# Choosing the best 80 tokens per expert of the first 16 tiles before attention has ended

## The chip, the cores and the metric

The kernel runs on one core of a Trainium2 chip. The metric is the time of one execution on the device in microseconds (us); smaller is better. The engines are TensorE (PE; its weight loads are PEld), VectorE (DVE), ScalarE (ACT), GpSimd (POOL) and SyncE (SP, which only issues transfers). Each works through its own queue in order.

## The reference

Sliding-window attention with sinks feeds a mixture of experts with a capacity.

```
q, k, v: [4, 8, 768, 64]        # 3072 tokens of 512 values come out of it
keep   = (key < 4) | (0 <= query - key < 128)
x      = softmax(where(keep, q @ k.T / 8, -1e9)) @ v     -> x[3072, 512]
logits = x @ w_gate                                      # [3072, 8]
expert = argmax(logits); gate_w = softmax(logits)[expert]
for e in 8 experts:
    tok = tokens of e; if more than 80: the 80 with the largest gate_w
    out[tok] = gate_w[tok] * (relu(x[tok] @ w1[e]) @ w2[e])   # w1 512x1024, w2 1024x512
out of every other token = 0
```

## The kernel before, in words

The 3072 tokens are 24 tiles of 128 rows. Attention runs in 48 ticks: a tick is two units of two heads, and four ticks make the rows of two tiles (at the end, two ticks make one tile). The kernel writes the order of the engines' instructions itself (`manual_schedule`): in tick n stand `scores(n)` on PE, `softmax(n)` on DVE and `exps(n)` on ACT, then `transposes(n-1)`, and `weighted(n-2)`, the product with v. A calendar (`at`, `run`) hangs the work of the finished tiles on later ticks: turning x back into rows (`rows_turn`, `rows_keep`, `rows_scale`) and writing them to DRAM (`rows_write`), the gate (`gate_products`, `gate_logits`, `gate_exp`, `gate_hit`, `gate_keys`), and the table from which tokens are later picked (`gate_picks`).

A token's key is its gate weight times a power of two of its expert, so that one comparison of keys ranks within an expert and between experts. For a tile i, `keys_turn` and `keys_keep` put its keys as a row into `krow`. `rank_compare` (DVE) compares the keys of tile i with `krow` in pieces of up to 768 columns, from column 0 to the tile's own end: each piece gives, per token, how many come before it (`parts`). The piece that holds the tile itself is a scalar_tensor_tensor with `ties` (L737), the others are tensor_scalars (L740). The same 0/1 matrix, summed over rows by a PE matmul (`rank_count`), gives the other direction, for the tokens of the columns. `rank_count_last` does that for the last tile with one-column matmuls.

After the last tick two drain ticks and a tail follow: the last tiles' gates, the remaining comparisons, the offsets of the experts (`owed`, `off`, `ot`, `os`), the rank of every token (L969), one-hot rows of the slots (`hot`, L974), 24 matmuls that pick token number and gate for 8 experts x 80 slots (`pi`, L977), the index (L985, L986) and eight indirect DMAs that gather the rows (L998). 14 matmuls (L996) run on PE while it waits. Then per expert: 64 + 64 matmuls of the first product (`ph`, L1042), 64 + 64 of the second (`py`, L1057), and an indirect DMA that scatters the result (L1085).

The weights are 32 tiles of 1 MB, each four transfers of 256 KB on SP's queue (`load_weight`, L296), in the order in which the experts need them. 6 tiles are loaded during attention. 7 get their memory from the q, k and v tiles when attention ends, 4 from its work tiles, and the last 15 wait for a tile that has been used up. SP issues a transfer only when the one eight places before it in its queue has landed.

## Time and profile before

| | |
|---|---|
| median of 3 runs | 322.52 us (322.12 to 324.51) |
| the profiled execution | 325.12 us, its span 323.4 us |
| first softmax of tick 34 and of tick 47 on DVE | 133.82 and 187.96 us |
| first gather starts | 219.73 us |
| first and last expert matmul | 227.72 and 316.7 us |
| busy: PE, DVE, ACT, POOL | 286.3, 180.4, 158.0, 165.7 us |

Times in rows are counted from the start of the span. A row of a timeline gives start, duration, engine, line, operation, output and inputs, and in brackets how long the engine was idle before it and what ended that.

### The profile page before, as it was taken

Reading aid. Unit: us, or ns where it says so; the run is one execution under the profiler, and the core shown is the slowest. Engines: PE = TensorE matmul, PEld = TensorE weight load, DVE = VectorE, ACT = ScalarE, POOL = GpSimd, SP = SyncE. Lnnn points to the kernel's source line nnn. Section 1 sums busy time; section 2 is a strip of 40 time slices with the busy share of each in tenths; the row PEclk is TensorE's granted clock in tenths of the full one; section 3 lists DMA queues with packets and bytes.
Section 4 is the critical chain, followed back from the end, with each engine's and each line's share of the span. In section 5 each row is a group of like instructions: output and inputs, shape, how many; then the busy total and the mean of one; then the engine's idle time right before and its main releaser. Section 6 shows DMA issues by size and latency. Waiting matters only on the chain.

```text
span 323.4 us, 10862 instructions
## 1 busy us (share of the span) xinstructions
PE 286.3 (89%) x4232; PEld 229.2 (71%) x4232; DVE 180.4 (56%) x576; ACT 158.0 (49%) x631; POOL 165.7 (51%) x365
## 2 busy tenths in 40 slices
PE   7498999999989999999999997556898999989992
PEld 2365787877767777877776675242887998978981
DVE  6355877696887888889989989970010000000000
ACT  0655797777877687867777562100011112111210
POOL 4396687758997587967676756616400110011002
PEclk9589999999999999999999999756799999999997
DMA  6999133599462799753450001999999697766801
GB/s 189 324 325 413 38 131 130 198 284 312 184 241 73 218 301 412 277 162 131 133 199 32 2 35 39 320 358 347 298 367 373 195 357 206 239 205 184 311 26 49
DMA packets 32745, 69.68 MB, mean 215 GB/s; under 512 B 4272, under 2 KB 5296, under 8 KB 32304
## 3 DMA queue, kind: packets, MB, share of 16 engines
q1 hardware_dynamic: 31376, 65.78, 61.0%
q0 software_dynamic: 1024, 2.62, 2.6%
q8 instruction: 35, 0.57, 0.7%
q10 hardware_dynamic: 288, 0.52, 0.4%
q14 instruction: 22, 0.18, 0.2%
HBM read 55.02 MB, written 13.89 MB: 213 GB/s over the span
## 4 chain that ended last, share of the span: by engine, by line
PE 59%; DVE 12%; ACT 9%; DMA 7%; issue 5%; POOL 5%; SPq 1%; POOLq 0%; DVEq 0%; ACTq 0%
PE ph L1042 12%; PE py L1057 12%; PE sc L499 11%; DMA w<-in_moe_w_dram 7%; PE xp L593 7%; PE pp L552 6%; ACT prob L536 5%; DVE gt L740 3%; PE pl L648 3%; ACT pt L564 2%; DVE sc L519 2%; DVE nm L526 2%; PE warm L412 1%; PE bank_t L754 1%; PE pr L622 1%
## 5 line engine op out<-in xcount | busy, mean ns | idle before, releaser
L536 ACT ACTIVATE prob<-sc,nm 128x132 f32<-128x132 f32 (+1 forms) x192 | 69.0, 377 | 4.6 <-DVE nm L526 4.3
L499 PE MATMUL sc<-k,q 64*128 64x260 f32 (+1 forms) x384 | 59.1, 411 | 8.7 <-ACT prob L536 8.2
L1085 POOL DMA_INDIRECT out_dram<-y,idx x8 | 7.4, 921 | 82.3 <-ACT y L1074 71.9
L564 ACT COPY pt<-pp 128x512 f32<-128x512 f32 x48 | 28.1, 586 | 41.3 <-PE pp L552 34.8
L499 PEld LDWEIGHTS sc<-k,q 64*128 64x128 f32 x384 | 30.5, 190 | 25.0 <-ACT prob L536 16.8
L1042 PE MATMUL ph<-xs,w 128*64 128x80 f32 x1024 | 40.0, 238 | 5.6 <-issue 4.4
L1030 DVE COPY xs<-px 128x320 f32<-128x320 f32 x8 | 3.9, 492 | 73.4 <-PE px L1028 65.2
L519 DVE COPY_PREDICATED sc<-upper,sc 128x256 f32<-128x256 int8 x80 | 33.7, 422 | 18.1 <-PE sc L499 9.5
L526 DVE TENSOR_REDUCE nm<-sc 128x2 f32<-128x264 f32 (+1 forms) x96 | 41.4, 431 | 3.3
L1042 PEld LDWEIGHTS ph<-xs,w 128*64 128x64 f32 x1024 | 38.3, 141 | 6.8 <-issue 6.0
L536 ACT ACTIVATION_READ_ACCUMULATOR prob<-sc,nm 128x1 f32 x192 | 40.6, 211 | 0.0
L1057 PE MATMUL py<-h,w 128*64 128x80 f32 x1024 | 38.3, 234 | 1.0 <-ACT yt L1065 0.6
L572 POOL TENSOR_SCALAR_AFFINE_SELECT own<-pt 128x512 f32<-128x512 f32 (+1 forms) x48 | 28.1, 585 | 21.2 <-ACT pt L564 20.4
L1057 PEld LDWEIGHTS py<-h,w 128*64 128x64 f32 x1024 | 36.5, 137 | 2.9 <-issue 2.1
L593 PE MATMUL xp<-pt,v 128*64 128x128 f32 x384 | 37.1, 286 | 0.0
L740 DVE TENSOR_SCALAR_CACHE_REDUCE gt<-krow,keys 128x768 bf16<-128x768 f32 x36 | 35.5, 1005 | 0.0
L552 PEld LDWEIGHTS pp<-ident,prob 128*128 128x128 f32 x192 | 20.8, 144 | 16.5 <-issue 11.8
L552 PE MATMUL pp<-ident,prob 128*128 128x128 f32 x192 | 32.3, 292 | 0.0
L593 PE MATMUL xp<-own,v 128*64 128x128 f32 x320 | 31.1, 273 | 0.0
L1044 ACT ACTIVATE h<-ph 128x320 f32<-128x320 f32 x16 | 7.0, 437 | 46.3 <-PE ph L1042 46.3
L579 POOL TENSOR_SCALAR_AFFINE_SELECT pt<-pt 128x512 f32<-128x512 f32 (+1 forms) x48 | 27.8, 579 | 3.3
L632 POOL TENSOR_TENSOR xr<-xr,rs 128x512 f32<-128x512 f32 x24 | 25.6, 1067 | 5.2 <-ACT xr L627 5.0
(136 smaller groups left out, 461.8 us busy)
## 6 DMA issues: line engine op xcount, KB each, us to landing
w<-in_moe_w_dram SPq DMA_DIRECT2D x128, 256.0 KB
v<-in_v_t_dram SPq DMA_DIRECT2D x12, 512.0 KB
out_dram<-zeros SPq DMA_DIRECT2D x24, 256.0 KB
q<-in_q_t_dram SPq DMA_DIRECT2D x11, 512.0 KB
x_rows<-xr SPq DMA_DIRECT2D x22, 256.0 KB
k<-in_k_t_dram SPq DMA_DIRECT2D x3, 1584.0 KB
k<-in_k_t_dram SPq DMA_DIRECT2D x1, 1056.0 KB
vst_raw<-in_vs_t_dram SPq DMA_DIRECT2D x4, 256.0 KB
```

The lines of the kernel that those rows point to most:

```text
L499: pe.matmul(sc[:, h, c0:c0 + w], qs[g][r, hp, j % 2 * P:(j % 2 + 1) * P], ks[b][r, hp, k0:k0 + w], start=True, stop=True)
L519: ve.copy_predicated(own, upper, sc[:, :, 0:P])
L526: ve.tensor_reduce(out=nm, in_=sc[:, :, lo_c:hi_c], axis=AX.X, op=ALU.max, negate=True)
L536: ac.activation(prob[:, a, h, p0:], sc[:, h, lo_c:hi_c], AF.Exp, bias=nm[:, h:h + 1], scale=1.0, accum_out=ssum[:, n, 2 * hp + h:2 * hp + ...
L552: pe.transpose(pp[:, a, h], prob[:, a, h, SINK:], ident)
L564: ac.copy(pt, st.pop((t, "pp")))
L572: po.affine_select(out=own[:, a0:], in_=pt[:, a0:], pattern=[[0, 2 - a0], [0, 2], [1, P]], compare_op=ALU.is_ge, fill=0.0, base=0, channel ...
L579: po.affine_select(out=pt[:, a0:], in_=pt[:, a0:], pattern=[[0, 2 - a0], [0, 2], [-1, P]], compare_op=ALU.is_gt, fill=0.0, base=0, channel ...
L593: pe.matmul(xp[h * D:(h + 1) * D, a * P:(a + 1) * P], val[:, (2 * hp + h) * D:(2 * hp + h + 1) * D], pr[:, a, h], start=False, stop=(a == ...
L740: ve.tensor_scalar(gt[:, 0:w], krow[:, c0:c0 + w], keys[:, i:i + 1], None, ALU.is_ge, ALU.add, accum_out=ra)
L1042: pe.matmul(ph[m * D:(m + 1) * D, f], columns(0, e, c, fc * P + m * D), x[:, c], start=(c == 0), stop=(c == DC - 1), skip_group_check=True)
L1057: pe.matmul(to[m * D:(m + 1) * D, dc], columns(1, e, k, dc * P + m * D), h[:, k], start=(k == 0), stop=(k == HC - 1), skip_group_check=True)
```

## The change

Tiles 0 to 15 (`CUT`) are ranked among themselves during ticks 34 to 42, and the best 80 per expert are chosen there: `kept_hot` (one-hot slots), `kept_pick` (16 matmuls), `kept_keys` (their keys from the picked gates) and `kept_row_turn` put the 640 chosen keys into `kept_row`. A later tile is compared with the columns from 2048 on and with the 640 columns of `kept_row`, and no longer with columns 0 to 2047. In ticks 34 to 38 up to three comparisons are made per tick (`quick`). The results on PE of these steps use the one PSUM tile of `transposes` (`spare`, tag pp). After tick 47 nothing is left to the calendar: the order of the last steps is written out, with the last rows stored from SP. The final choice adds 8 matmuls over the kept tokens to 8 over the new tiles. Before the gather 4 weight tiles are loaded; the fifth is asked for behind the first gather, and a 1x1 memset on POOL, written behind that gather, stands before it. The core of the diff:

```diff
+    CUT = 16
+    NNEW, C0, HALF = NTILE - CUT, CUT * P, E // 2 * CAP
-    def load_weight():
+    def load_weight(hold=False):
...
+        if hold:
+            po.memset(t[0:1, 0:1], 0.0)
         to = t.rearrange("p (c f) -> p c f", c=src.shape[1])
         for i in range(0, 2 * F, DM):
...
         def keys_keep(i0, nb):
             ac.copy(krow[:, i0 * P:(i0 + nb) * P], gst.pop((i0, "pk"))[:, 0:nb * P])
             for i in range(i0, i0 + nb):
-                for c in range((i * P) // PIECE + 1):
-                    rank_todo.append((i, c))
+                lo = 0 if i < CUT else C0
+                todo = [(i, n, c, min(c + PIECE, (i + 1) * P)) for n, c in enumerate(range(lo, (i + 1) * P, PIECE))]
+                if i >= CUT:
+                    todo.append((i, NPC - 1, None, None))
+                rank_todo.extend(todo)
...
+            if c0 is None:
+                ve.tensor_scalar(gt[:, 0:E * CAP], kept_row, keys[:, i:i + 1], None, ALU.is_ge, ALU.add, accum_out=ra)
...
+        def spare(nm):
+            return ps_p.tile([P, 512], F32, tag="pp", name=nm)
+        def kept_hot():
...
+            for i0 in range(0, CUT, CUT // 2):
+                i1 = i0 + CUT // 2
+                ve.tensor_tensor(hot[:, i0:i1], slot_row[:, None, :].to_broadcast([P, i1 - i0, CAP]),
+                                 rank[:, i0:i1, None].to_broadcast([P, i1 - i0, CAP]), ALU.is_equal)
+        def kept_pick():
...
+            for t in range(CUT):
+                pe.matmul(pi, hot[:, t], picks[:, t], start=(t == 0), stop=(t == CUT - 1))
+        def kept_row_turn(n):
+            row = spare(f"kept_row_{n}")
+            for e in range(E // 2):
+                pe.transpose(row[:, e * CAP:(e + 1) * CAP], kept["key"][:, ...].to_broadcast([CAP, P]), ident[0:CAP, 0:CAP])
...
+        at((K0 + 6, "pe end"), count_ahead, "owed0", range(CUT))        # K0 = 31
+        at((K0 + 8, "act mid"), keep_counts, -(-C0 // CROW))
+        at((K0 + 8, "pe end"), kept_turn)
+        at((K0 + 8, "dve end"), kept_hot)
+        at((K0 + 9, "pe end"), kept_pick)
+        at((K0 + 9, "act end"), kept_keep)
+        at((K0 + 10, "pool"), kept_keys)
+        for n in range(2):
+            at((K0 + 10 + n, "pe end"), kept_row_turn, n)
+            at((K0 + 10 + n, "act end"), kept_row_keep, n)
...
-                for _ in range(min(left, 3) if n >= NTK else -(-left // 3)):
+                quick = K0 + 3 <= n <= K0 + 7
+                for _ in range(min(left, 3) if quick else -(-left // 3)):
                     rank_compare()
...
+            gate_picks(g0, 2)                     # POOL, tiles 20 and 21; g0 = 20, i = 23
+            compare(g0, 0)
...
+            rows_turn(g0, 1)
+            rows_keep(g0, 1)
+            rows_scale(g0, 1)
+            rows_write(g0, 1, nc.sync)
+            gate_products(i, 1)
+            for _ in range(2):
+                load_weight()
...
+            rows_write(i - 1, 0, nc.sync)
...
+            rows_keep(i, 0)
+            rows_scale(i, 0)
+            rows_write(i, 0, nc.sync)
+            for _ in range(2):
+                load_weight()
...
+            keys_turn(i, 1)
+            keys_keep(i, 1)
+            for n in (NPC - 1, 0, 1):
+                compare(i - 1, n)
+            rank_count()
+            owed = misc("owed")[:, 0:E]
...
+            kept_hots = const.tile([CAP, E, CAP], BF16, name="kept_hots")
...
-        for n in range(NC):
-            load_weight()
...
             po.indirect_dma_start(out=xg[e], out_offset=None, in_=x_rows, ...)
+            if e == 0:
+                load_weight(hold=True)
+        while len(wtiles) < NA + NB + NC:
+            load_weight()
```

The order that comes out of it differs at three places. DVE, from the logits of tiles 14 and 15 in tick 35 to the softmax of tick 37 (`sc` and `nm` are a softmax, `gt` a comparison). Before:

```order
L661 TENSOR_TENSOR ls_2336<-lg_2334,mx_2335 128x16
L737 SCALAR_TENSOR_TENSOR gt_2_2356,parts<-krow,keys,ties 128x128
L740 TENSOR_SCALAR gt_0_2358,parts<-krow,keys 128x768
...
L682 TENSOR_SCALAR keys,un_14_2407<-gate,cm_all 128x1 x2
L740 TENSOR_SCALAR gt_1_2427,parts<-krow,keys 128x768
L615 TENSOR_SCALAR rs_2437,un_2438<-sum_2123 128x16
L616 RECIPROCAL rs_2437<-rs_2437 128x16
L516 COPY_PREDICATED sc_0_2429<-upper_160,negc 128x2x128
```

and now:

```order
L700 TENSOR_SCALAR keys,un_14_2377<-gate,cm_all 128x1 x2
L764 TENSOR_SCALAR gt_0_2380,parts<-krow,keys 128x768
L764 TENSOR_SCALAR gt_1_2382,parts<-krow,keys 128x768
L761 SCALAR_TENSOR_TENSOR gt_2_2384,parts<-krow,keys,ties 128x256
L526 COPY_PREDICATED sc_0_2391<-upper_163,negc 128x2x128
```

Three comparisons stand between two softmaxes where one or two stood. DVE behind the last softmax, from the last tiles' comparisons to the index. Before:

```order
L740 TENSOR_SCALAR gt_0_3489,parts<-krow,keys 128x768
L740 TENSOR_SCALAR gt_1_3491,parts<-krow,keys 128x768
L943 TENSOR_REDUCE os<-ot 128x24
L946 TENSOR_TENSOR parts<-parts,ct 128x24
L740 TENSOR_SCALAR gt_2_3502,parts<-krow,keys 128x768
L737 SCALAR_TENSOR_TENSOR gt_3_3522,parts<-krow,keys,ties 128x768
L951 TENSOR_TENSOR parts<-parts,last 128x23
L969 TENSOR_REDUCE rank<-parts 128x24
L974 TENSOR_TENSOR hot<-slot_row,rank 128x640 x3
```

and now:

```order
L756 TENSOR_SCALAR gt_3_3472,parts<-kept_row,keys 128x640
L1119 TENSOR_REDUCE os<-ot 128x8
L764 TENSOR_SCALAR gt_0_3504,parts<-krow,keys 128x768
L1134 TENSOR_TENSOR kept_rank<-kept_rank,spare_m 80x8
L1135 TENSOR_TENSOR kept_rank<-kept_rank,spare_3294 80x8
L1137 TENSOR_TENSOR kept_hots<-slot_row,kept_rank 80x640
...
L761 SCALAR_TENSOR_TENSOR gt_1_3519,parts<-krow,keys,ties 128x256
L1148 TENSOR_TENSOR parts<-parts,spare_3293 128x7
L1164 TENSOR_REDUCE rank<-parts 128x8
L1172 TENSOR_TENSOR hot<-slot_row,rank 128x320 x2
```

The last tile has three comparisons for four, two `hot` of 320 columns stand for three of 640, and three operations on the kept tokens come in. SP, from the store of tile 20 on (`w_3_0` is the first half of a weight of expert 3; `xr_1_3363`, `xr_0_3389` and `xr_0_3410` are the rows of tiles 21, 22 and 23). Before, where tiles 22 and 23 are stored from ACT's queue:

```order
L636 DMA x_rows<-xr_0_3184 128x512
L636 DMA x_rows<-xr_1_3320 128x512
L296 DMA w_2_0_3348<-in_moe_w_dram 128x512 x4
L296 DMA w_2_1_3353<-in_moe_w_dram 128x512 x4
L296 DMA w_1_0_3358<-in_moe_w_dram 128x512 x4
L296 DMA w_1_1_3363<-in_moe_w_dram 128x512 x4
```

and now:

```order
L654 DMA x_rows<-xr_0_3250 128x512
L302 DMA w_3_0_3608<-in_moe_w_dram 128x512 x3
L302 DMA w_3_1_3635<-in_moe_w_dram 128x512 x4
L654 DMA x_rows<-xr_1_3363 128x512
L302 DMA w_2_0_3375<-in_moe_w_dram 128x512 x4
L302 DMA w_2_1_3380<-in_moe_w_dram 128x512 x4
L654 DMA x_rows<-xr_0_3389 128x512
L302 DMA w_2_0_3640<-in_moe_w_dram 128x512 x2
L654 DMA x_rows<-xr_0_3410 128x512
...
L302 DMA w_2_1_3645<-in_moe_w_dram 128x512 x4
L302 DMA w_3_0_3608<-in_moe_w_dram 128x512
L302 DMA w_4_0_3650<-in_moe_w_dram 128x512 x4
```

Of the tile that is held, `w_3_0_3608`, three quarters stand ahead of tile 21's rows; the quarter that the memset touches stands behind 31 quarters of weights.

## Rows read from the trace of the kernel before

**Rows 1.** Windows, core 0: stretch, its length, busy time (instructions) by engine, PEclk, DMA share, GB/s.

```profile
133.82:187.96 54.14, 52.08 (x588) 39.84 (x584) 49.67 (x157) 38.00 (x159) 38.22 (x90) 1.00 0.36 116
189.57:217.39 27.82, 18.57 (x203) 13.04 (x201) 26.04 (x85) 7.31 (x26) 14.11 (x42) 0.81 0.57 197
219.73:227.72 7.99, 5.06 (x17) 2.31 (x16) 0.49 (x1) 0.00 (x0) 6.16 (x7) 0.71 1.05 329
227.72:316.72 89.00, 83.00 (x2106) 79.02 (x2106) 3.44 (x7) 14.95 (x31) 8.67 (x11) 0.98 0.76 247
```

**Rows 2.** Timeline of PE: the scores of two ticks, four ticks apart.

```profile
114.51 1.15 PE L499 MATMUL sc<-k,q 64*128 64x260 f32 x8
...
129.31 1.15 PE L499 MATMUL sc<-k,q 64*128 64x260 f32 x8
```

**Rows 3.** Timeline of DVE: first softmax of ticks 34, 37, 38 and 47.

```profile
133.82 0.43 DVE L519 COPY_PREDICATED sc<-upper,sc 128x256 f32<-128x256 int8 x1 [1.24 <-PE sc L499]
...
146.64 0.41 DVE L516 COPY_PREDICATED_SCALAR sc<-upper,negc 128x256 f32 x1
...
149.16 0.48 DVE L516 COPY_PREDICATED_SCALAR sc<-upper,negc 128x256 f32 x1
...
187.96 0.43 DVE L519 COPY_PREDICATED sc<-upper,sc 128x256 f32<-128x256 int8 x1 [0.48 <-PE sc L499]
```

**Rows 4.** Timeline of DVE: a softmax with sinks to its end, a tile pair's gate.

```profile
142.23 0.48 DVE L516 COPY_PREDICATED_SCALAR sc<-upper,negc 128x256 f32 x1
...
144.15 0.39 DVE L672 SCALAR_TENSOR_TENSOR eq_all<-ls,p_bits 128x16 f32<-128x16 f32 x1
...
189.57 0.28 DVE L657 TENSOR_TENSOR t<-pl,rs 128x128 f32<-128x128 f32 x1
...
191.99 1.01 DVE L740 TENSOR_SCALAR_CACHE_REDUCE gt<-krow,keys 128x768 bf16<-128x768 f32 x1
```

**Rows 5.** DVE, tail: the whole-width comparisons by shape: line, names, shapes, count, busy us, mean ns, idle.

```profile
L740 DVE TENSOR_SCALAR_CACHE_REDUCE gt<-krow,keys 128x768 bf16<-128x768 f32 x13 | 12.8, 1004 | 0.0
```

**Rows 6.** Timeline of DVE: the end of the comparisons.

```profile
207.61 1.00 DVE L740 TENSOR_SCALAR_CACHE_REDUCE gt<-krow,keys 128x768 bf16<-128x768 f32 x1
208.55 0.87 DVE L737 SCALAR_TENSOR_TENSOR gt<-krow,keys,ties 128x640 bf16<-128x640 f32 x1
...
209.35 1.00 DVE L740 TENSOR_SCALAR_CACHE_REDUCE gt<-krow,keys 128x768 bf16<-128x768 f32 x1
```

**Rows 7.** Timeline of DVE: waits and one-hot rows of the choice.

```profile
211.59 0.35 DVE L943 TENSOR_REDUCE os<-ot 128x24 f32<-128x192 f32 x1 [0.29 <-POOL ot L935]
...
214.30 0.20 DVE L951 TENSOR_TENSOR parts<-parts,last 128x23 f32<-128x23 f32 x1 [0.39 <-PE last L764]
...
215.10 2.29 DVE L974 TENSOR_TENSOR hot<-slot_row,rank 128x640 bf16<-128x640 f32 x3
```

**Rows 8.** Timeline of PE: the first gathered rows are turned.

```profile
226.59 0.50 PE L1028 MATMUL px<-ident,xg 80*128 80x80 f32 x4 [2.30 <-DMA xg<-x_rows,idx_in]
```

**Rows 9.** Timeline of POOL: the first gather.

```profile
219.73 1.22 POOL L998 DMA_INDIRECT xg<-x_rows,idx_in  x1 [7.46 <-DMA w<-in_moe_w_dram]
```

**Rows 10.** Gathers (first row) and scatters (second): microseconds from issue to landing.

```profile
DMA to landing us min/median/max: 6.9/7.1/7.3
...
DMA to landing us min/median/max: 2.6/2.9/6.6
```

**Rows 11.** Timeline of POOL: a row scaling, end of a pair's picks.

```profile
194.00 1.04 POOL L632 TENSOR_TENSOR xr<-xr,rs 128x512 f32<-128x512 f32 x1
...
196.88 0.56 POOL L709 TENSOR_TENSOR picks<-onehot,g 128x16 bf16<-128x16 f32 x3
```

**Rows 12.** Timeline of ACT: a tile's rows copied out of PSUM.

```profile
199.41 0.59 ACT L627 COPY xr<-pr 128x512 f32<-128x512 f32 x1
```

**Rows 13.** DVE: one operation beside the scaling, and its smaller form by shape.

```profile
194.06 1.01 DVE L689 TENSOR_TENSOR ahead<-cm_all,p_bits 128x16 bf16<-128x16 f32 x1
...
L689 DVE TENSOR_TENSOR ahead<-cm_all,p_bits 128x8 bf16<-128x8 f32 x2 | 0.3, 172 | 0.0
```

More of the change, by code (lines that the diff above doesn't have):

```diff
@@ L732, in rank_compare @@
[L732 to L737 removed]
+            i, n, c0, c1 = rank_todo.pop(0)
+            gt = wk.tile([P, PIECE], BF16, tag="gt", name=f"gt_{i}_{n}", bufs=NGT)
+            ra = parts[:, i, n:n + 1]
@@ L765, in rank_count_last, with count_ahead, kept_offsets @@
                               stop=True, skip_group_check=True)
             rank_done.clear()
+        def spare(nm):
+            return ps_p.tile([P, 512], F32, tag="pp", name=nm)
+        kept = {}
+        def count_ahead(nm, tiles):
+            to = spare(nm)[:, 0:E]
+            for n, t in enumerate(tiles):
+                pe.matmul(to, ones_bf, ahead[:, t], start=(n == 0), stop=(n == len(tiles) - 1))
+            kept[nm] = to
+        def kept_offsets():
+            off = sm.tile([P, E], F32, name="off0", bufs=1)
+            ac.copy(off, kept.pop("owed0"))
+            kept["off"] = off
@@ new lines, in attention_moe, with keep_counts, turn_counts, kept_turn @@
+        NM = CROW // P
+        crow = sm.tile([P, CROW], F32, name="crow", bufs=1)
+        def keep_counts(rows):
+            ac.copy(crow[64:64 + rows], counts[64:64 + rows])
+        def turn_counts(to, rows):
+            for m in range(NM):
+                pe.transpose(to[:, m * rows:(m + 1) * rows], crow[64:64 + rows, m * P:(m + 1) * P],
+                             ident[64:64 + rows, 64:64 + rows])
+        def kept_turn():
+            rows = -(-C0 // CROW)
+            kept["ct"] = spare("ct0")[:, 0:NM * rows]
+            turn_counts(kept["ct"], rows)
@@ L768, in attention_moe, with kept_row_keep @@
+        def kept_row_keep(n):
+            row = kept.pop("row")
+            ac.copy(kept_row[:, n * HALF:(n + 1) * HALF], row[:, 0:HALF])
+            if n == 1:
+                ac.copy(kept_ahead, row[:, HALF:HALF + E])
         cal = {}
@@ L900, in attention_moe, with compare @@
-                n += 1
-            now[0] = n
-            i = NTILE - 1
+                n += 1
+            cal.clear()
+            now[0] = NTK
+            t, i = NTK - 1, NTILE - 1
+            g0 = i - 3
+            def compare(i, n):
+                k = [x[:2] for x in rank_todo].index((i, n))
+                rank_todo.insert(0, rank_todo.pop(k))
+                rank_compare()
+            sink_probs(t)
+            transposes(t)
+            keep_probs(t)
+            weighted(t - 1)
@@ new lines, in attention_moe @@
+            gate_experts(g0, 2)
+            gate_picks(g0, 2)
+            compare(g0, 0)
+            gate_hit(i - 1, 1)
+            gate_keys(i - 1, 1)
+            weighted(t)
+            keep_x(t)
+            lctx.close()
+            wpool2 = fast.enter_context(tc.tile_pool(name="wpool2", bufs=1, side="right", reuse_waits="tile"))
+            homes += [(wpool2, m) for m in range(NB)]
+            rows_turn(g0, 1)
+            rows_keep(g0, 1)
+            rows_scale(g0, 1)
+            rows_write(g0, 1, nc.sync)
@@ L919, in attention_moe @@
-            rank_todo.clear()
             keys_keep(i, 1)
-            rank_todo[:0] = held
-            rows_write(i, 0, ac)
-            while rank_todo[0][0] < i:
-                rank_compare()
-                rank_count()
-            crow = sm.tile([P, CROW], F32, name="crow", bufs=1)
-            ac.copy(crow[64:72], counts[64:72])
-            owed = misc("owed")[:, 0:E]
-            for m in range(NTILE):
-                pe.matmul(owed, ones_bf, ahead[:, m], start=(m == 0), stop=(m == NTILE - 1))
@@ L952, in attention_moe @@
-            assert not cal and not rank_done, cal
+            for n in (NPC - 1, 0, 1):
+                compare(i - 1, n)
+            rank_count()
+            owed = misc("owed")[:, 0:E]
+            for m in range(CUT, NTILE):
+                pe.matmul(owed, ones_bf, ahead[:, m], start=(m == CUT), stop=(m == NTILE - 1))
+            off = sm.tile([P, 2, E], F32, name="off", bufs=1)
+            ac.copy(off[:, 0], owed)
+            rows = 10
+            keep_counts(rows)
+            po.tensor_tensor(off[:, 1], off[:, 0], kept_ahead, ALU.add)
@@ new lines, in attention_moe @@
+            po.tensor_tensor(base[:, CUT:], later[:, CUT:], os, ALU.subtract)
+            gate_picks(i - 1, 2)
+            last = misc("last")
+            rank_count_last(last)
+            ct = misc("ct")
+            turn_counts(ct, rows)
+            c0 = NM * rows
+            for c in range(E // 2):
+                pe.transpose(ct[0:CAP, c0 + c * rows:c0 + (c + 1) * rows], crow[64:64 + rows, c * CAP:(c + 1) * CAP],
+                             ident[64:64 + rows, 64:64 + rows])
+            compare(i, 0)
@@ L954, in attention_moe @@
+            assert not rank_done and not rank_todo
     with ExitStack() as fctx:
```

258 lines of the change are left out of this document (166 added, 92 removed).

## The prediction, made before the changed kernel ran

> **What bounds the kernel now.** I read the windows by stage first, then the timelines at the edges of the stages, then the places where an engine waits. The profiled execution took 325.12 us, 2.6 above the median of 322.52; its span is 323.4, so 1.7 lie outside. All sums below are made within it, and the difference that comes out is taken off the median.
>
> Three stretches matter [rows 1]. From the softmax of tick 34 (133.82) to that of tick 47 (187.96, called T0) DVE is busy 49.67 of 54.14 us and PE 52.08. Which one sets the pace is seen from the ticks before: where DVE has few comparisons, the scores of four ticks go by in 129.31 - 114.51 = 14.80, 3.70 a tick [rows 2]; here a tick takes 4.16 on the mean. So DVE, with its comparisons, sets it, and PE's own pace is a floor 0.46 lower. A tick with nothing but a softmax can catch up: 2.52 from tick 37 to 38 [rows 3]. In the second stretch, 189.57 to 217.39, DVE is busy 26.04 of 27.82: the work behind attention is a chain on DVE, broken by waits of 0.29, 0.39 and a few small ones [rows 1, 7]. Then index, gather (it starts at 219.73, T0 + 31.77 [rows 9]) and 7.1 us until its rows land [rows 10]; PE has stood still for 2.30 by then [rows 8]. The last stretch is the experts: PE is busy 83.00 of 89.00 at a granted clock of 0.98 [rows 1]. The change leaves it the same matmuls, and I move it as a block.
>
> **Term 1, ticks 34 to 46: -0.5.** Prices: a softmax 1.61 (187.96 to 189.57), one with sink columns 1.92 (142.23 to 144.15), the gate of a pair of tiles 2.42 (189.57 to 191.99) [rows 3, 4]; a comparison of 768 columns 0.93 from start to start (207.61 to 208.55), one of 640 columns 0.80 (208.55 to 209.35) [rows 6], so about 0.13 for each 128 columns less. By the new order DVE does in tick 35 1.61 + 2.42 + 2 x 0.93 + 0.41 = 6.3; tick 36 about 4.8 (1.92, three comparisons of 2.4, the rest small); tick 37 4.5; tick 38, without a comparison, 2.4; tick 39 about 5.5, with two one-hot rows of 0.76 (a third of 2.29 [rows 7]). Tick 34 stays 4.24, since PE sets it. That is 27.7 for six ticks. The seven behind them have fewer comparisons (640 columns for 2048), so PE's 3.70 sets them: 25.9. Sum 53.6 for 54.14, -0.5. The new work on PE (16 pick matmuls, the turns of the keys) stands against comparison matmuls that fall away, and I count it at nothing; uncovered it is at most 3 us, by the floor of 0.46 a tick over seven ticks (3.2). On the other side, if ticks 37 and 38 catch up as in [rows 3], up to 3 are gained. Bounds -3 and +3.
>
> **Term 2, DVE behind attention: -5.7.** Comparisons now: 13 of 768 columns [rows 5] x 0.93 = 12.1, and five with ties (256 to 768 columns) 0.41 + 0.54 + 0.67 + 0.80 + 0.93 = 3.4; 15.5. Afterwards the order has five of 640 against the kept keys (4.0), two of 768 (1.9) and four with ties, 640, 768, 128 and 256 (2.4): 8.3, so -7.2. The one-hot rows were three of 640 (2.29) and become two of 320 (0.76): -1.5. Added are `kept_hots` (0.76 as one of 640), two small subtractions (0.4) and two more corrections of `parts` (0.2): +1.4.
>
> A wait is added. `xr` has two buffers, so the ACT copy of tile 23's rows stands until tile 21's rows have left for DRAM, and behind it on ACT stand tile 23's `krow`, `crow` and `off`; PE's `pk` for tile 23 waits with it (same bank), then the counts, `owed`, and POOL's `ot`, for which DVE waits at `os`. POOL scales tile 21 behind the picks of tiles 20 and 21, which took from 195.04 to 197.44 [rows 11], so the store is issued at about T0 + 11.5. With the shortest landing of this kind and size, 2.6 [rows 10], and the copy of 0.59 [rows 12], and 2.6 for the counts and the small steps behind them (an estimate), `os` comes at T0 + 17.3, while DVE has done all else by about T0 + 15.2: 2.1 idle, and 0.7 for the two known waits on PE, 2.8 for 1.1 before: +1.7. Bounds: 0 if the landing were free (-7.4 in all), +4.5 more if the store lands like a gather in a busy queue, 7.1 [rows 10]; I take the short end, as the stretch before T0 + 15 has little traffic besides. Sum -7.2 - 1.5 + 1.4 + 1.7 = -5.6; with -0.1 for fewer small waits -5.7.
>
> **Term 3, SP and the gather: 0.** SP now stores tiles 20 to 23. 31 quarters of weights (7.75 MB) stand ahead of the quarter that waits for the memset, 7 of them ahead of tile 21's rows. At the 329 GB/s of the gather's stretch [rows 1] a quarter (256 KB) takes 0.8: the last rows land by about T0 + 23, the queue is drained about T0 + 30. The gather, which waits for those rows, starts at T0 + 26, so it still runs into weights: the hold covers almost none of it, and I leave 7.1 as it is. The memset stands behind the first gather and delays only SP's later weights; their need lies 20 us and more ahead. The edges of this term: -4.2 if the gather lands in 2.9, like a scatter [rows 10], +1 if a gather and the weights meet worse than now.
>
> The sum is -6.2: 318.9 for the profiled execution, **316.2 for the median**. Its own range, from the bounds that are likely (-3.5 to +3), is 312.5 to 319.
>
> **A rule against it.** DVE's operation on 128x16 at 194.06 took 1.01 beside a POOL row scaling that ran from 194.00 to 195.04, where the form of half its width takes 0.17 [rows 11, 13]. Behind attention three such scalings (tiles 21, 22, 23) remain, and the new order puts operations of two inputs nearer to them, since fewer comparisons (one input) are left as a cover. In the kernel before one of them cost 0.84 (1.01 - 0.17); if each of the three now costs its whole 1.04, that is 3.1 - 0.8 = +2.3. I take none of it in the sum. The Trainium skill, page SBUF - State Buffer, section SBUF: two separate sides, says that a DVE operation with two inputs from SBUF and a GpSimd operation hold a shared pair of ports in turn, each for its whole length. By that rule the trace agrees at this place.
>
> **The rivals.**
> - The hold works, or the queue is drained sooner: the gather lands in 2.9, and PE's clock stays up (the experts' stretch shows 0.98; 0.02 of 89 is 1.8 us): -4.2 - 1.8, 310.2. For it: four places on SP wait for rows, and the quarters ahead of them may go early. Against it: the 31 quarters. 13%.
> - The late store: tile 21's rows land 7.1 behind their issue, because seven quarters of weights stand directly ahead: +4.5, 320.7. For it: these quarters and the new place on SP. Against it: three of the seven go into memory that is free well before and may have landed by then. 9%.
> - The port: +2.3, 318.5. 7%.
> - The choice ahead pays nothing, since another chain (keys of tile 23, counts, offsets) has the same end: about 322, 6%. Against it: DVE is busy 94% of that stretch [rows 1].
> - Slower: the kept steps share the one PSUM tile of the transposes, so that in ticks 37 to 42 a tick's transposes must wait until ACT or DVE has read the result of a kept step. It decides from 1.2 us a tick over five ticks, where term 2 is used up; at 2.2 each it is +11 and the time 327. For it: PE is busy 52.08 of 54.14 there, so little can be hidden [rows 1]. Against it: such a result is at most 640 columns, and one copy takes 0.59 [rows 12]. 6%.
>
> The forecast has the remaining 59%. Low end 309.5, below the rival with the hold; high end 320.5, which leaves out about half of the late store, no gain, and slower. A change of less than 1% (3.2 us) can't be told from none. Faster by over 1%, below 319.3: 58 of the forecast, 13, 6 of the port, 1 of the late store, 0.78. Slower by over 1%: 0.06. The same: 0.16.
>
> **What will show it.** In the changed trace: the softmax of tick 47 between 187 and 188.5; ticks 35 and 39 longer than 5 us, the last seven close to 3.7; no comparison of `krow` columns below 2048 in the tail, five of 640 with 0.8 each; an idle time of about 2 us before `os`, with ACT's copy of tile 23 behind a DMA; the first gather at T0 + 26, and 7 us until it lands; the experts 89 us as before. The forecast is wrong if the tail is no shorter than 24 us, if ticks 37 to 42 grow on PE's waits for ACT, or if the gather's landing differs from 7.1 by more than 2.

## The result, and the profile of the changed kernel

The changed kernel took 318.25 us (median of 4 runs, 317.17 to 319.62), the kernel before 322.32 beside it (322.11 to 324.51): a ratio of 0.986, 95% interval 0.981 to 0.991. That is faster by 4.1 us; 6.2 were forecast, and 318.25 lies within the range.

The two profiled executions are further apart than the medians, 325.12 and 317.17: that of before is slower than the four runs beside the change, that of after the fastest of its four. By stages:

| stage, us | before | forecast | after |
|---|---|---|---|
| start to the softmax of tick 34 | 133.82 | the same | 134.24 |
| ticks 34 to 46 | 54.14 | 53.6 | 55.82 |
| softmax of tick 47 (T0) to the first gather | 31.77 | 26.1 | 26.09 |
| first gather to the first expert matmul | 7.99 | 8.0 | 8.09 |
| experts, to the start of the last two transposes | 89.47 | the same | 84.90 |
| of these, idle time of PE that nothing in the profile ended ("issue"; called stalls) | 4.84 | | 1.25 |

Of the 7.9 us between the two spans (323.4 and 315.5), 3.6 are such stalls in the experts, which differ from execution to execution and are followed up below. Ticks and tail together, +1.7 and -5.7, are -4.0, the size of what the medians show. That these two stretches make the whole difference of the medians is argued: of the kernel before there is one trace only.

The windows of after, for [rows 1] and the two halves of the ticks (length, busy PE, PEld, DVE, ACT, POOL with instructions, PEclk, DMA share, GB/s):

```profile
134.24:162.84 28.60, 26.14 (x299) 19.30 (x296) 27.00 (x80) 18.36 (x77) 19.29 (x48) 1.00 0.45 144
162.84:190.06 27.22, 27.08 (x332) 22.04 (x330) 20.11 (x75) 20.51 (x88) 20.31 (x47) 1.00 0.23 79
191.68:213.14 21.46, 14.35 (x164) 11.17 (x160) 18.46 (x73) 7.41 (x26) 13.22 (x34) 0.79 0.75 248
216.15:224.24 8.09, 3.75 (x16) 1.81 (x14) 0.49 (x1) 0.00 (x0) 6.35 (x8) 0.71 1.06 337
224.24:309.14 84.90, 82.31 (x2106) 78.83 (x2107) 3.77 (x8) 15.01 (x32) 8.52 (x11) 0.98 0.79 257
```

In ticks 34 to 39 DVE is busy 27.00 of 28.60; in ticks 40 to 46 PE is busy 27.08 of 27.22, DVE only 20.11. So the bound changes sides in the middle of the loop. Before, the same two groups of ticks took 24.19 and 29.95 us: the first has become 4.4 longer, the second 2.7 shorter. The new matmuls on PE in the second half (by shape: count, busy us, mean ns, idle before):

```profile
L773 PE MATMUL bank_t<-gt,pick_row 128*128 128x320 bf16 x6 | 1.3, 299 | 0.0
L893 PE MATMUL kept_row<-ident,kept_key 80*128 80x80 f32 x8 | 1.0, 245 | 0.0
L870 PE MATMUL pi<-picks,hot 128*80 128x40 bf16 x16 | 0.8, 194 | 0.0
L897 PE MATMUL kept_row<-kept_before,ones_bf 80*128 80x8 bf16 x8 | 0.3, 166 | 0.0
```

The last three, 2.1 us, are the kept choice; the first are counts of the new comparisons with the kept keys. On DVE (timeline) two ticks of the first half, and a wait that the order put there:

```profile
138.48 0.43 DVE L529 COPY_PREDICATED sc<-upper,sc 128x256 f32<-128x256 int8 x1
...
144.98 0.48 DVE L526 COPY_PREDICATED_SCALAR sc<-upper,negc 128x256 f32 x1
...
153.66 1.27 DVE L761 SCALAR_TENSOR_TENSOR gt<-krow,keys,ties 128x512 bf16<-128x512 f32 x1
...
173.80 0.88 DVE L756 TENSOR_SCALAR_CACHE_REDUCE gt<-kept_row,keys 128x640 bf16<-128x640 f32 x1 [1.77 <-ACT kept_row L903]
```

Tick 35 takes 6.50 (138.48 to 144.98; 6.3 were worked out); tile 15's comparison of 512 columns takes 1.27. The tail, DVE first, for [rows 7, 13]:

```profile
200.26 0.23 DVE L675 TENSOR_TENSOR t<-spare,rs 128x64 f32<-128x64 f32 x1 [0.80 <-ACT xr L645]
...
201.65 1.87 DVE L761 SCALAR_TENSOR_TENSOR gt<-krow,keys,ties 128x768 bf16<-128x768 f32 x1
...
208.29 0.22 DVE L1119 TENSOR_REDUCE os<-ot 128x8 f32<-128x64 f32 x1 [0.73 <-POOL ot L1114]
...
212.25 0.89 DVE L1172 TENSOR_TENSOR hot<-slot_row,rank 128x320 bf16<-128x320 f32 x2
```

POOL, ACT and PE, for [rows 8, 9, 11, 12]:

```profile
200.66 2.05 POOL L650 TENSOR_TENSOR xr<-xr,rs 128x512 f32<-128x512 f32 x2
...
216.15 1.21 POOL L1196 DMA_INDIRECT xg<-x_rows,idx_in  x1 [4.36 <-DMA x_rows<-xr]
```

```profile
204.90 0.59 ACT L645 COPY xr<-spare 128x512 f32<-128x512 f32 x1 [2.87 <-DMA x_rows<-xr]
...
214.20 0.17 ACT L1187 COPY tab<-pi 80x24 f32<-80x24 f32 x1 [0.23 <-DVE idxf L1183]
```

```profile
222.86 0.79 PE L1230 MATMUL px<-ident,xg 80*128 80x80 f32 x4 [3.76 <-DMA xg<-x_rows,idx_in]
```

`os` comes at T0 + 18.2 (T0 + 17.3 forecast), the gather at T0 + 26.09; its rows are turned 6.7 us later, and PE now waits 3.76 for it, where it waited 2.30. SP (timeline; start, length of a run of issues, count):

```profile
201.73 0.33 SPq L654 DMA_DIRECT2D x_rows<-xr  x1
202.10 4.18 SPq L302 DMA_DIRECT2D w<-in_moe_w_dram  x8
206.38 0.66 SPq L654 DMA_DIRECT2D x_rows<-xr  x1
207.07 2.33 SPq L302 DMA_DIRECT2D w<-in_moe_w_dram  x2
209.81 0.33 SPq L654 DMA_DIRECT2D x_rows<-xr  x1
```

The rows of tile 23 are scaled by 206.60, but SP issues them at 209.81, behind weights, and the gather is released by their landing: it starts 1.95 behind `tab` (the last small copy on ACT ahead of it), where 1.08 lay between them before.

### The profile page after: what moved, and what is told of

Read it like the earlier page. It is cut to its first block, busy times and chain, and to the rows that moved or that the text cites. A ratio compares the mean times of both kernels' runs of the same rounds, so it can differ in the third digit from the quotient of the medians.

```text
span 315.5 us, 10856 instructions
## 1 busy us (share of the span) xinstructions
PE 282.3 (90%) x4233; PEld 228.7 (73%) x4233; DVE 170.2 (54%) x562; ACT 158.9 (50%) x637; POOL 166.9 (53%) x364
## 4 chain that ended last, share of the span: by engine, by line
PE 60%; DVE 12%; ACT 9%; POOL 7%; DMA 6%; issue 4%; SPq 1%; POOLq 0%; DVEq 0%; ACTq 0%
PE ph L1244 12%; PE py L1259 12%; PE sc L509 12%; PE xp L603 7%; PE pp L562 6%; DMA w<-in_moe_w_dram 6%; ACT prob L546 4%; DVE gt L764 2%; ACT pt L574 2%; PE pl L666 2%; DVE sc L529 2%; DVE nm L536 2%; PE warm L419 2%; PE pr L640 2%; POOL xr L650 1%
## 5 line engine op out<-in xcount | busy, mean ns | idle before, releaser
L603 PEld LDWEIGHTS xp<-pt,v 128*64 128x64 f32 x384 | 21.4, 137 | 3.5 <-POOL pt L589 0.2
```

The costliest lines, as they stand in the source:

```text
L603: pe.matmul(xp[h * D:(h + 1) * D, a * P:(a + 1) * P], val[:, (2 * hp + h) * D:(2 * hp + h + 1) * D], pr[:, a, h], start=False, stop=(a == ...
```

## The experiments

All are the changed kernel with one edit; e8 takes over that of e3, e10 and e11 put several together, and e12 is the change itself. "Ticks" are ticks 34 to 46, "tail" is T0 to the first gather, "to px" the first gather's issue to the first transpose of its rows (`px`), "stalls" PE's idle time in the experts that nothing in the profile ended. The stretches are from the one profiled execution of each run. The kernel before was timed again beside each group of runs, and the ratio is to those times.

| run | median us (runs) | ratio to before, 95% | ticks | tail | to px | experts | stalls |
|---|---|---|---|---|---|---|---|
| the change | 318.25 (4) | 0.981 to 0.991 | 55.82 | 26.09 | 6.71 | 84.90 | 1.25 |
| e1_hold_all | 319.09 (6) | 0.985 to 0.995 | 55.81 | 25.27 | 4.99 | 90.90 | 7.16 |
| e2_xr3 | 318.17 (6) | 0.981 to 0.991 | 55.82 | 26.10 | 6.83 | 88.26 | 3.70 |
| e3_kept_late | 318.04 (6) | 0.981 to 0.991 | 56.08 | 26.25 | 6.86 | 85.63 | 2.15 |
| e4_act_store | 320.53 (12) | 0.990 to 0.998 | 55.81 | 27.92 | 7.41 | 84.83 | 0.48 |
| e5_nohold | 318.59 (4) | 0.983 to 0.996 | 55.81 | 26.56 | 6.83 | 85.77 | 2.04 |
| e6_no_late_weights | 315.17 (4) | 0.971 to 0.983 | 55.81 | 26.53 | 6.80 | 82.80 | 0 |
| e7_half | 336.60 (6) | 1.040 to 1.049 | 55.81 | 25.48 | 4.99 | 106.32 | 0 |
| e8_spread | 318.87 (12) | 0.985 to 0.993 | 55.01 | 26.23 | 6.64 | 86.68 | 2.18 |
| e9_six_pieces | 317.64 (6) | 0.980 to 0.990 | 55.82 | 25.28 | 6.04 | 90.48 | 0.65 |
| e10_xr3_spread | 316.53 (6) | 0.980 to 0.990 | 55.01 | 26.11 | 7.02 | 86.62 | 2.34 |
| e11_xr3_hold_six | 322.84 (12) | 0.996 to 1.004 | 55.82 | 26.12 | 5.04 | 91.18 | 2.04 |
| e12_change_again | 317.68 (6) | 0.982 to 0.993 | 55.80 | 26.24 | 6.86 | 86.21 | 1.39 |

Edits behind the ticks leave them at 55.80 to 55.82. The stretch ahead of tick 34, which no edit touches, repeats less well: it takes 132.2 to 134.5 us in these traces. So the totals of two single traces can differ by 2 us without any doing of the edit.

**e1_hold_all: does the hold work if all the weights behind it are held?**

```diff
-        chain.enter_context(tc.manual_schedule(engines={ve.engine, po.engine}))
+        chain.enter_context(tc.manual_schedule(engines={ve.engine, po.engine, nc.sync.engine}))
```

> SP's queue is put under the written order, so that 16 quarters of weights stand ahead of the held one and the other 15 that had been moved up stand behind it. Theory A (the gather lands late because weights are in its way, and the hold as changed covers nothing): the queue is empty at the gather, it lands in about 3 us instead of 7.0, the first px comes up to 4 us earlier, the experts do not wait for weights: about 314.3 us, 4 less than the change. Rival B (7 us is the gather's own length, or the held weights are then late for experts 1 to 3): the landing stays at 6 us or more, or PE waits for w in the experts; 318 to 321 us.

The gather lands 4.9 us behind its issue, the tail is 0.8 shorter (the stores no longer stand behind moved-up weights, and the gather starts 1.25 behind `tab`), and the first expert matmul comes at T0 + 31.3, 2.8 earlier than T0 + 34.2. None of it is left at the end: the experts take 90.90, with 7.16 of stalls. Theory A had the direction right (the first px comes 2.5 us earlier, not 4) and the end wrong. Its empty queue did not come about either: SP issues nothing from 212.03 to 214.65, but the DMA engines work on (share 1.00 from 213.0 to 218.5). Rival B named the weights, but no wait for w is in the trace. Its gathers:

```profile
213.31 1.21 POOL L1196 DMA_INDIRECT xg<-x_rows,idx_in  x1 [3.66 <-DVE idx L1185]
...
DMA to landing us min/median/max: 4.9/7.8/9.0
```

and what PE waits for ahead of and in its experts (line, releaser, us in total, times, longest):

```profile
PE ph L1244 <- issue: 4.8, 6, 1.4
PE py L1259 <- issue: 2.3, 3, 1.5
PE px L1230 <- DMA xg<-x_rows,idx_in: 1.5, 1, 1.5
```

A second gain comes with the early landing. PE waits 1.5 us for the gathered rows instead of 3.76, and its granted clock then stays at its upper level (2.4 GHz), where in the change it is at the lower one (1.2 GHz) until 228.1. The same stretch, from the first expert matmul to the second expert's rows, in the change and in e1:

```profile
224.24:231.73 7.49, 6.91 (x132) 6.66 (x132) 0.49 (x1) 0.88 (x2) 2.08 (x4) 0.74 1.06 302
219.38:225.04 5.66, 5.08 (x133) 4.83 (x133) 0.49 (x1) 0.88 (x2) 3.48 (x6) 1.00 1.05 284
```

That is 1.83 us. So 4.7 us are won by then (2.8 and 1.8), and the stalls behind it cost more.

What "issue" is here can be read from the trace's records of the transfers. The page of the change lists a queue of instructions:

```profile
q8 instruction: 35, 0.57, 0.7%
```

35 packets of 16 KB, and 4233 matmuls with as many weight loads: one for some 120 matmuls. That they are PE's is inferred from their times. In e1 each stall ends 2.2 to 2.8 us behind the start of such a packet:

```
packet starts     226.28 233.07 238.32 243.86 249.29 255.24 260.75 271.23 292.09
PE goes on        229.09 235.71 240.81 246.46 251.87 257.80 263.21 273.47 294.48
difference          2.81   2.64   2.49   2.60   2.58   2.56   2.46   2.24   2.39
```

In the change the two stalls end 2.58 and 2.42 behind a packet's start (238.01 and 252.70); in the trace of before six of the seven do so (2.4 to 2.6), the seventh, of 0.39, does not. So PE seems to have run out of instructions at these places and to wait for the next 16 KB. Whether these are asked for late or queue behind weights is not shown; they are late where the DMA engines are full, in e1 for 40 us of the experts (DMA share 1.05), in the change for 20:

```profile
219.38:239.38 20.00, 16.54 (x436) 15.85 (x438) 0.98 (x2) 2.18 (x5) 3.48 (x6) 1.00 1.05 337
239.38:259.38 20.00, 17.97 (x457) 16.83 (x453) 0.98 (x2) 3.55 (x7) 1.88 (x2) 1.00 1.05 384
```

```profile
224.24:244.24 20.00, 18.33 (x435) 17.67 (x437) 0.98 (x2) 2.17 (x5) 2.08 (x4) 0.90 1.04 348
244.24:264.24 20.00, 19.80 (x518) 18.91 (x514) 0.98 (x2) 3.97 (x8) 1.88 (x2) 1.00 0.85 277
```

The Trainium skill, page DMA: Bandwidth & Descriptors, section Issuing engines are not separate DMA queues, says that transfers started by the scalar, sync and gpsimd engines run on the same 16 DMA engines and interleave there. The trace agrees: in e1 packets of the gathers and of the weights start side by side in every microsecond from 216 to 228. The instructions are a third queue beside them (q8).

**e6_no_late_weights: are the stalls the weights' doing?**

```diff
         which, e, half = wsrc[n]
+        if n >= NA + NB + NC:
+            wtiles[wsrc[n]] = wtiles[wsrc[n - 15]]
+            return
```

> The 15 weight tiles from the 18th on are not loaded; their products use tiles that are already there. So no weights move during most of the experts, which start no earlier. Theory A (the PE stalls of the experts that the trace gives no releaser for, 0.5 to 7.2 us by run, are fetches of PE's own instructions behind weight transfers): the stalls go to under 0.5 us from the point on where the last weight has landed, and from there the experts go at the pace of the stretches without a stall (about 10.3 us per expert, 83.5 in all): 316 to 317.5. Rival B (the stalls come from PE itself, or from waits on weights that are not shown): with the weights gone they stay at 2 us or more (B1), or experts get faster by more than the stalls (B2, under 315).

With no weights under way the stalls are gone, all of them; PE is busy to the last hundredth for 20 us at a time:

```profile
244.30:264.30 20.00, 20.00 (x543) 19.44 (x539) 0.98 (x2) 4.16 (x9) 1.87 (x2) 1.00 0.07 20
```

The same 16 instruction packets start in the experts as in e1 and in the change. That decides for theory A against B1. The experts take 82.80; the change without its stalls has 83.65, so the experts got faster by 0.85 more than the stalls, which is B2's sign, and the time of 315.17 lies between A's range and B2's. The traces, set beside each other matmul by matmul from start to start, account for the 0.85: of the 2.10 us that the experts of the change are longer than those of e6, 2.1 arise at places 2.3 to 2.7 us behind a packet's start, and nothing over 0.1 anywhere else. The profile counts a part of each such pause as busy time of the last matmul before it, so its 1.25 is too small. By the same count e1 loses 9.5 us at its packets, and its fast first stretch gives back 1.6; the trace of before loses 6.3, which is 4.2 more than the change and most of the 4.57 by which the two profiles' experts differ.

**e2_xr3: the wait of ACT for a free `xr`.**

```diff
-            xr = wk.tile([P, H, D], F32, tag="xr", name=f"xr_{i0}_{n}")
+            xr = wk.tile([P, H, D], F32, tag="xr", name=f"xr_{i0}_{n}", bufs=3)
```

> The row tile xr gets a third buffer, so that ACT's copy of tile 23's rows no longer waits for the store of tile 21 (2.87 us in the changed kernel). Theory A (that wait sits on the chain krow, counts, off, os, but the gather is released by the landing of tile 23's rows at 216.15, behind the weights on SP): os comes 0.7 us earlier, the gather does not: 318.0 to 318.4. Rival B (the chain through os decides the gather): up to 1 us faster than the change, 317.3.

The time and the start of the gather are those of theory A, the way there is not. ACT no longer waits, but `os` comes at T0 + 18.95, 0.7 later than in the change (T0 + 18.23). DVE and POOL of e2 show why:

```profile
199.89 1.87 DVE L761 SCALAR_TENSOR_TENSOR gt<-krow,keys,ties 128x768 bf16<-128x768 f32 x1
...
201.69 0.99 DVE L690 SCALAR_TENSOR_TENSOR eq_all<-ls,p_bits 128x8 f32<-128x8 f32 x1
...
207.26 0.22 DVE L1119 TENSOR_REDUCE os<-ot 128x8 f32<-128x64 f32 x1 [0.88 <-POOL ot L1114]
```

```profile
198.90 3.76 POOL L650 TENSOR_TENSOR xr<-xr,rs 128x512 f32<-128x512 f32 x3
```

Three row scalings now run without a gap until 202.66. DVE's `eq_all` of tile 23, an operation of two inputs that takes 0.16 in the change, now takes 0.99 and ends with them; tile 23's keys, the counts and `os` hang on it. In exchange tile 23's rows are stored earlier, and the gather starts 1.25 behind `tab` instead of 1.95. So 0.7 is lost and 0.7 won.

**e3_kept_late: the wait for `kept_row` in tick 42.** The comparisons with `kept_row` are left aside until tick 43:

```diff
+        SH = 0
...
+        def rank_next():
+            ks = [k for k, x in enumerate(rank_todo) if x[2] is not None or now[0] >= K0 + 12 + SH]
...
-                    rank_compare()
+                    rank_next()
```

> The comparisons with the kept keys begin one tick later (tick 43), so that DVE does not stand 1.77 us in tick 42 for the second half of kept_row. Theory A (that wait lengthens tick 42, 4.86 us, and the loop with it): the softmax of tick 47 comes 1.0 to 1.5 us earlier, about 317 us. Rival B (PE works through tick 42 without a pause, 4.83 us from scores to scores, and sets it): tick 47's softmax stays within 0.4 us and so does the time, 318.

The wait of 1.77 is gone and the ticks take 56.08 for 55.82. The softmax of tick 43 waits 1.79 for PE's scores instead. Rival B.

**e8_spread: the choice one tick later, its comparisons over six ticks.**

```diff
-                quick = K0 + 3 <= n <= K0 + 7
-                for _ in range(min(left, 3) if quick else -(-left // 3)):
-                    rank_compare()
+                quick = K0 + 3 <= n <= K0 + 7 + SH
+                for _ in range(min(left, {35: 2, 37: 2, 38: 2}.get(n, 3)) if quick else -(-left // 3)):
+                    rank_next()
```

`SH` is 1 here and is added to the tick of each kept step too; `rank_next` is that of e3.

> The steps that choose among tiles 0 to 15 come one tick later and their comparisons are spread over six ticks, at most 2 in ticks 35, 37 and 38; the kept comparisons begin in tick 44. Theory A (the loop grew because DVE's comparisons are bunched in ticks 35 to 37, 6.5, 5.0 and 4.9 us each, while later ticks leave it idle): ticks 34 to 46 take 54.5 us or less instead of 55.8, the tail grows by up to 0.8 for kept comparisons that move into it: about 317.3. Rival B (PE's own work sets the 13 ticks: 53.2 us busy of 55.8, with or without the bunch): the 13 ticks stay at 55.3 to 56, the tail grows, 318.5 to 319.

The ticks take 55.01, 0.8 less: between the two theories. The bunch on DVE is a part of the loss; with it spread PE is busy 52.9 of 55.0. The edit also moves tile 15's comparison away from an operation of POOL that it met before (below): it takes 0.67 here, 1.20 in the change. Which of the two the 0.8 comes from is not separated. The time is 318.87 in 12 runs, no gain.

**e4_act_store: tiles 22 and 23 stored from ACT's queue.**

```diff
             rows_scale(i - 1, 0)
-            rows_write(i - 1, 0, nc.sync)
...
             gate_exp(i, 1)
+            rows_write(i - 1, 0, ac)
...
             rows_scale(i, 0)
-            rows_write(i, 0, nc.sync)
...
             ac.copy(off[:, 0], owed)
             rows = 10
+            rows_write(i, 0, ac)
```

> The rows of tiles 22 and 23 are stored from ACT's queue instead of SP's, tile 22's behind gate_exp of tile 23, tile 23's behind off. Theory A (tile 23's rows land late, 6.3 us behind their issue at 209.81, because they stand behind weights on SP, and the gather waits 0.9 us for them): the store is issued at about 208.1, lands before the index is there, and the gather starts 0.5 to 0.9 us earlier: about 317.5. Rival B (a store meets the same transfers from whichever queue it is issued): it lands as late, the gather starts within 0.3 us of the change's: 318.2.

Both were wrong. The rows were in time (the gather starts 1.25 behind `tab`), but `tab` is 2.5 later:

```profile
210.07 0.33 ACTq L654 DMA_DIRECT2D x_rows<-xr  x1
210.44 0.47 ACT L836 COPY crow<-bank_t 10x384 f32<-10x384 f32 x1 [2.74 <-POOL gr L720]
```

```profile
211.83 0.16 DVE L1134 TENSOR_TENSOR kept_rank<-kept_rank,spare_m 80x8 f32<-80x8 f32 x1 [2.27 <-PE spare_m L1128]
```

The rows were scaled by 206.75, `off` was copied by 207.71, and the issue still waited until about 210. The trace's records show for what: ahead of the issue stands a wait of ACT, until 210.01, for the semaphore on which this store is going to report, and a weight that SP issued at 204.31 reported its landing on the same one at 209.99. The stores and the weights use the same eight semaphores in turn, so a store waits for a transfer eight places before it from either queue. Behind it on ACT stands `crow`, and DVE waits 2.27 for what comes of that.

**e5_nohold: no memset.**

```diff
-                load_weight(hold=True)
+                load_weight()
```

> The 1x1 memset behind the first gather is left out, so no weight is held. Theory A (31 quarters stand ahead of the held one, the queue is never empty at the memset, so the hold does nothing): gather 7 us from issue to landing, start at T0 + 26, time within 1 us of the change, 318.2. Rival B (the hold keeps some weights out of the gather's way): the gather lands 1 to 3 us later than 7.0 and the time is 319 to 321.

To px 6.83 for 6.71, the time within the runs of the change: the hold as changed does nothing that is seen.

**e7_half and e9_six_pieces: smaller transfers.** In e7 all eight, in e9 two of the four transfers of a late weight tile are cut in half:

```diff
-        for i in range(0, 2 * F, DM):
+        w = DM if n < NA else DM // 2
+        for i in range(0, 2 * F, w):
...
-            nc.sync.dma_start(to[:, c, f:f + DM], src[:, c, f:f + DM])
+            nc.sync.dma_start(to[:, c, f:f + w], src[:, c, f:f + w])
```

(the edit of e7; that of e9 is of the same kind)

> Weight tiles from the seventh on are loaded in transfers of 128 KB instead of 256, so that the eight which SP has under way are 1 MB instead of 2. Theory A (what a gather or an instruction fetch waits for is the bytes under way: 2 MB at 329 GB/s is 6.2 us, close to the 7.0 that the gather takes): the gather lands in 4 to 4.5, px comes 2.5 to 3 us earlier and PE's stalls in the experts shrink: 314 to 316. Rival B (SP needs 0.46 us for each issue, so 128 KB come at 285 GB/s at most; the experts then wait for weights): PE waits for w, 319 or more. Rival C (the gather's 7 us are its own): landing unchanged at 6.5 to 7.3, 318.

> Two of a weight tile's four transfers are cut in half (128 KB), for the tiles from the seventh on, so that SP's issues (0.5 to 0.6 us each) let through about 300 to 340 GB/s instead of the 385 at which the DMA engines were full. Theory A (PE's instruction fetches are late only while the engines are full; a small gap between transfers lets them through): the stalls without a releaser fall under 0.5 us, the gather lands a little earlier (5.5 to 6.5), no waits for w: 316 to 317. Rival B (SP's limit starves the later experts, as with eight transfers per tile): waits for w appear, 319 to 325. Rival C (transfers of 1 KB rows are slower by themselves and fill the engines as much): stalls as before and time 318 to 319.

In e7 the gather lands in 4.9, so about 2 us of its 7 are a wait for the bytes ahead of it, and there is no stall; but SP's 185 last issues take 109.0 us, 0.59 each, 222 GB/s, and PE waits 13.5 us for weights: 336.6.

```profile
PE py L1260 <- DMA w<-in_moe_w_dram: 8.7, 13, 1.6
PE ph L1245 <- DMA w<-in_moe_w_dram: 4.8, 3, 1.9
```

In e9 stalls are down to 0.7, and 2.6 of waits for w have come in; the median is that of the change. A and B both hold in part. Its profile is of its slowest run (319.53), and its experts (90.48) are longer by more than these waits. Behind the longest of them PE's granted clock is at its lower level, and 100 matmuls take 6.58 us, where 64 take 2.44 at the upper one:

```profile
298.53 6.58 PE L1261 MATMUL py<-h,w 128*64 128x80 f32 x100 [1.67 <-DMA w<-in_moe_w_dram]
...
298.50:302.00 3.50, 3.47 (x52) 3.47 (x54) 0.00 (x0) 0.00 (x0) 0.00 (x0) 0.50 1.00 291
```

So a wait for weights costs more than its length, in e7 and e11 too: there the clock falls to 0.50 at 277.99 and at 292.13, each time in or just behind such waits.

**e10_xr3_spread and e11_xr3_hold_six: put together.** e10 is e2 and e8, e11 is e1, e2 and the cut of e9.

> The third xr buffer and the spread choice together: the trace of each had a shorter stretch ahead of the experts (0.8 us in the tail by the buffer, 0.8 us in ticks 34 to 46 by the spread). Theory A (what comes before the experts adds up and is kept): 316.5 to 317.2. Rival B (experts that start earlier meet more weight traffic and give it back in late instruction fetches): the experts start 1 to 1.6 us earlier, PE's stalls there grow by as much, 318 to 319.

> SP in the written order (16 quarters before the held tile, nothing moved up), third xr buffer, and six transfers per late weight tile. Theory A (the experts' start 3.7 us earlier, seen with the order alone, is kept once fetches get through the weights): gather at T0 + 24.0 to 24.5, landing 5 or less, stalls under 2 us instead of 7.2, 314 to 315.5. Rival B (the weights, held back and then at 300 to 340 GB/s, are late): waits for w of 3 us or more, 318 to 322.

e10 keeps the 0.8 of the ticks and, as in e2 (whose tail of 26.10 does not show the 0.8 that the expectation credits it with), nothing of the buffer (tail 26.11); it stalls 2.34 in the experts. Its 316.53 (315.71 to 318.76) is the lowest median of all that compute the whole, 6.1 below before; its interval and that of the change cover each other, so that it beats the change is not shown. e11 lands its gather in 5.0 and stalls 2.04, but one wait for w takes 2.9, and its experts 91.18: 322.84, no better than before and close to rival B.

**e12_change_again: the change once more.**

> The changed kernel once more, unchanged, for a second profile and more times beside the kernel before. Theory A (everything ahead of the experts repeats, and PE's stalls on instruction fetches in the experts differ from execution to execution): ticks 34 to 46 take 55.6 to 56.0, the gather starts at T0 + 26.0 to 26.6 and lands in 7.0, the experts take 83.7 us plus stalls, which come out other than the 1.25 us of the first profile (0.5 to 4), and the time follows them; median 317.5 to 318.8. Rival B (the stalls belong to the kernel): 1.0 to 1.5 us again at the same two places. Rival C (the stretches ahead of the experts are what varies): ticks or tail differ by over 0.7 us from the first profile.

Ticks 55.80, tail 26.24, landing 6.9, as A had them. Not all ahead of the experts repeats, though: tick 34 begins at 132.39 for 134.24. Stalls 1.39 at three places for 1.25 at two: the sum as rival B had it. The experts without them are 84.82 for 83.65, 1.1 over theory A's 83.7. The six times go from 316.92 to 320.92, and the profiled one is the fastest again; whether the slower ones are longer by stalls stays open, since they have no trace.

## Why the prediction was right, and where it was not

**Term 1 (-0.5; measured +1.7) failed**, at the step "the seven behind them have fewer comparisons, so PE's 3.70 sets them", and with it "I count it at nothing". PE does set them, but at 3.89 (27.22 for seven): the stretch from which 3.70 was read holds none of the kept choice, and its 2.1 us of matmuls (0.8, 1.0, 0.3) stand on an engine that is busy 27.08 of 27.22. The comparison matmuls that fell away could not pay for it, because most of them were missing from that quiet stretch already: 1.7 us in its four ticks, 1.8 now in seven, 5.7 in these seven before. They were counted twice, once in the 3.70 and once against the new work. That is +1.3 of the miss of 2.2. The other 0.9 is in ticks 34 to 39, 28.60 for 27.7: tile 15's comparison took 1.20 from start to start for the 0.67 of the sum, and tick 38 waits 0.56 for PE. Beside that comparison ran POOL's `ot`, which took 0.89; in e8, where the two do not meet, they take 0.67 and 0.46. Spreading the work took 0.8 off (e8). The wait of 1.77 that stands out in DVE's timeline was worth nothing (e3): DVE was not the bound in that tick.

**Term 2 (-5.7; measured -5.7) was right in its sum, and not in each part.** The wait before `os` is 0.73 for 2.1: the chain behind tile 21's store came 0.9 later than forecast, but DVE's own work 2.3 later (T0 + 17.5 for T0 + 15.2). In that stand a wait of 0.80 for ACT before DVE's `t` and 1.7 of the port (below); and 0.9 came in at the gather, for tile 23's rows. What made up for them is the stretch from `os` to the gather, 7.9 for 8.8 with those 0.9 in it. No run shows which part of the sum was too high there. That the errors cancel to 0.0 is luck.

**Term 3 (0) was right:** 31 quarters (transfers of 256 KB) stand ahead of the held one, the gather lands as before, and without the memset nothing changes (e5).

**The rival of the port was right for the most part.** A comparison of 768 columns with ties took 1.80 beside POOL's scaling for 0.93, one of 128 columns 0.54 for 0.27, and `ls` before them 0.71 for 0.17: +1.7 of the 2.3 given, in a sum that came out nevertheless. The 0.5 of tile 15 in tick 37 is of the same kind, at a place where the prediction did not look for it. e2 shows it as a cause: take away ACT's wait, and the scaling that moves up blocks DVE. The Trainium skill, page SBUF - State Buffer, section SBUF: two separate sides, has the rule that such a pair of operations takes turns whole; the trace agrees (0.99 for 0.16, 1.87 for 1.01). Comparisons with one input, such as the 640 columns at 0.80 each, kept their time.

**The late store** came with tile 23, not with tile 21: 6.3 us from issue to the gather it releases, and 0.9 of it on the path. **The rival of a hold that works** was tried in e1: its mechanism is true (landing 4.9, and 1.8 by the clock, the 1.8 that the rival gives), its price of -6.0 is not: the first stretches gain 4.7 in all, and the experts give it back at the instruction packets. **The rival of the shared PSUM tile** did not come: from 144 to 190 us PE waits 2.3 us in all, none of it ahead of a transpose.

**"I move it as a block"** is a step that was weaker than it looked: with weights in transfers of 256 KB the experts are 83.5 to 84.8 us (82.8 without late weights) and PE's stalls, 0.5 to 7.2 in these traces, least where the experts start latest (e4), most where the weights are held and the start comes early (e1). The trace of before held 4.84 of them, which is the larger part of why the two profiles differ by twice what the medians do; that its execution is long for this reason is likely, but there is no second trace of that kernel.

Two small slips in the prediction's sums decide nothing: 322.52 less 6.2 is 316.3, not 316.2, and its own range begins at 312.8, not 312.5.

## What to carry to other kernels

Read an engine's floor from the ticks that the change alters, with the work that it adds, not from a quieter stretch, or count only what the quieter stretch still holds as falling away; and of two engines within a few per cent of each other, count new work on either in full. A gain ahead of a stage that shares the DMA engines with its own supply is only a gain when that stage's supply comes no later: look at the stage's length after each edit, not only at its start. A wait next to a slow neighbour engine may be a rest that the neighbour fills: removing it can move a blocked operation into its place.

## What the runs showed of the hardware

- The instruction queue moved 35 packets of 16 KB, one for some 120 matmuls. With the DMA engines full of weights PE stood for 0.2 to 2.0 us at such places, and went on 2.2 to 3.0 us behind a packet's start. With no weights under way it did not stand at all (e6), nor with 1 MB of them instead of 2 (e7).
- Of the first gather's 7 us, 2 are queue: it lands in 4.9 with 1 MB under way (e7), and when SP has issued nothing for the 1.3 us before it and the 1.3 behind it (e1). What the other 4.9 are is open: the DMA engines were at a share of 0.9 to 1.0 in both.
- SP issued 0.59 us apart in e7; transfers of 128 KB then carried 222 GB/s.
- A DVE operation of two inputs, 0.16 by itself, took 0.99 beside a POOL scaling (e2).
- A store from ACT's queue was issued when a weight from SP's queue had landed on the semaphore that both use, 2.3 us after what is before it on ACT had ended (e4).
- PE's granted clock was 0.74 over the first 7.5 us of the experts where PE had stood 3.76 us for the gather (the change), and 1.00 where it had stood 1.5 (e1): 1.8 us.
